# Moving state products, query transposes, output rows, table reads, squares and gates to other places in a retention and expert kernel

## The chip, the cores and the metric

The kernel runs on one core of a Trainium2 chip. The metric is device time of one execution in microseconds, median over the runs. Engines are named PE (TensorE's products), PEld (its weight loads), DVE (VectorE), ACT (ScalarE), POOL (GpSimd) and SP (SyncE, which here issues transfers); POOL issues the indirect transfers. PSUM banks hold TensorE's results.

## The reference

A linear attention with decay over 4 batches, 8 heads, 768 positions and 64 columns a head gives 3072 rows x of 512 columns. Each row chooses the expert with the largest cosine logit of eight, and passes through that expert's two layers (512 to 1024 to 512) with a gate.

```python
for t in range(S):
    state = gamma * state + k[:, :, t] (outer) v[:, :, t]
    y[:, :, t] = scale * q[:, :, t] @ state
x = y.transpose(0, 2, 1, 3).reshape(B * S, H * D)
logits = normed(x) @ normed(expert_emb).T / tau
expert_idx = argmax(logits);  gate_w = softmax(logits)[expert_idx]
for e in range(E):
    h = maximum(x[mask] @ w1[e], 0)
    out[mask] = gate_w[mask] * (h @ w2[e])
```

## The kernel before, in words

**Order.** All five engines run under a manual schedule: each executes its instructions in the order in which the code writes them, so moving a line moves its instructions past everything that the same engine, or the same transfer queue, does in between. An instruction that waits holds up all behind it on its engine.

**Attention.** 12 steps m (4 batches by 3 blocks of 256 positions) run in one loop. A step has two halves s of keys. For each: the product of keys and queries (`scores`, L357, banks psc), a product of the queries with the running state (`inter`, L410, banks py), VectorE's `masks` (L366) over the scores, and the product of masked scores and values (`intra`, L410). `state(m)` (L382) adds a block's keys times values into the banks pst, ACT's `state_copy` copies one of them, and VectorE's `state_sums` (L394 to L399) makes the state that the next step's `inter` reads. `transpose_k` and `transpose_q` (L330) turn the next step's keys and queries on TensorE into one of two banks pt; ACT copies them (L340, L346). `take` has ACT copy the step's result from py (L432); in the next step `logits_products` (L451) multiplies it with the turned embeddings, and `rows` turns it on VectorE (L437) and writes it to the x rows in DRAM (xd).

**Routing.** Steps are gathered in groups; when a group is over, `sums` (L469), `choose`, `count` (L496 to L500) and `ranks` find each row's expert and its place, and POOL's `place` writes the entries of 128 rows with one indirect transfer each (L529) into a table tbl in DRAM. Expert 0's first 288 rows ("early") are read from the table at step 10 and gathered (`early_gather`, L559, tile xge); the other 128 ("late", tile xr0) can be read only when the last group is placed.

**Weights.** An expert has eight pieces of 512 KB. `load_piece` (L183 to L191) starts the transfer of the next piece on SP into one of 3 tiles raw (pool rp). `split_cast` has ACT round it to whi (L210) and `low` has VectorE subtract to wlo (L215); `split` does both. Each product is three: xh with whi, xl with whi, xh with wlo. The tuples `LOADS` and `SPLITS` name the steps at which pieces are started and split during the attention.

**Experts.** `rows_T` (L577, L580) turns gathered rows of expert 0 on TensorE; for experts 1 to 7 rows are gathered (`gather_rows`, tile xr), written to DRAM scratch xs (`write_rows`) and read back in quarters (`read_quarters`, L912, tile xg), turned on VectorE and rounded (`x_turn`, L922 and L923), and `x_low` (L929) makes xl. `next_x(e, i)` does that for the next expert in three parts during the second layer, each with a weight split. `first_layer` (L228) and `hidden` (L234 on ACT, L235 on VectorE) give hh and hl; `layer2` (L939) and, for experts with 384 rows, `layer2_rows` (L981) give the output, which `finish` scales by the gate (L956) and POOL writes out (L963). `squares` (L262, ACT) and `gates` (L246 to L283, VectorE with one POOL instruction, L247, and one ACT instruction, L277) make the gates. `run(n)` puts the next n products of expert 0's first layer into the tail of the routing.

## Time and profile before

| | us |
|---|---|
| median of 3 runs | 455.42 |
| lowest and highest run | 452.3, 456.49 |
| the profiled execution, whole | 450.94 |
| its span in the trace | 449.1 |
| busy time of PE, DVE, ACT, POOL in it | 411.2, 255.5, 173.8, 168.7 |
| mean granted clock of TensorE | 0.975 |

The profiled execution lies 4.48 us under the median of the runs; 1.84 us of it lie outside the traced span. The granted clock is a share of full speed, of 2.4 GHz: 0.50 is 1.2 GHz. "Idle before" is time in which an engine stood, and the arrow names what ended it.

### The profile page before, as it was taken

To read this page: it belongs to the slowest core of one execution; us is meant where nothing else is said; L and a number is where in the kernel's file an instruction comes from. 1 tells how busy PE (TensorE), PEld (TensorE's weight loads), DVE (VectorE), ACT (ScalarE), POOL (GpSimd) and SP (SyncE) were. 2 spreads that over 40 slices of the span, in tenths; PEclk is the share of its full clock that TensorE was granted. 3 is DMA by queue.
4 is the path that set the end of the run, shared out by engine and by line. 5 is a ranking of instruction groups with operands and counts; after the bars stand their busy time and mean duration, and the time that the engine had idled before them with its cause. 6 is when DMAs were issued, how large, how long until landed. Compare 5 with 4: busy or idle time off the path is not lost.

```text
span 449.1 us, 11335 instructions
## 1 busy us (share of the span) xinstructions
PE 411.2 (92%) x4540; PEld 367.0 (82%) x4540; DVE 255.5 (57%) x543; ACT 173.8 (39%) x315; POOL 168.7 (38%) x171
## 2 busy tenths in 40 slices
PE   7889889998859979997999999999998997999993
PEld 4778767877636978896899999999998987989982
DVE  3454745655862925565856585378467558666410
ACT  3314333334342515345346346156237326525300
POOL 1743356665645242072440172143135065012011
PEclk9989999999996999999899999999999999999998
DMA  9998878888583468649886968778788697864001
GB/s 238 274 227 217 224 196 228 222 217 200 131 228 112 99 165 234 151 122 279 233 267 176 229 220 243 165 254 268 177 242 273 178 290 256 257 203 138 0 26 47
DMA packets 97966, 88.75 MB, mean 198 GB/s; under 512 B 11148, under 2 KB 79644, under 8 KB 97904
## 3 DMA queue, kind: packets, MB, share of 16 engines
q1 hardware_dynamic: 92832, 74.85, 62.6%
q0 software_dynamic: 4928, 13.04, 8.4%
q8 instruction: 37, 0.61, 0.6%
q14 instruction: 25, 0.20, 0.2%
q10 hardware_dynamic: 144, 0.05, 0.1%
HBM read 65.27 MB, written 18.87 MB: 187 GB/s over the span
## 4 chain that ended last, share of the span: by engine, by line
PE 38%; DMA 16%; SPq 15%; DVE 10%; issue 10%; POOL 6%; ACT 4%; POOLq 0%; DVEq 0%; ACTq 0%
SPq L951 8%; PE py L410 5%; DMA xg<-xs 5%; PE py L981 5%; PE psc L228 4%; PE pt L330 4%; PE pst L228 4%; DMA xr<-xd,gi 4%; PE psc L357 4%; DVE wlo L215 3%; PE py L228 3%; DMA xs<-xr 2%; PE psc L939 2%; ACT whi L210 2%; SPq L912 2%
## 5 line engine op out<-in xcount | busy, mean ns | idle before, releaser
L215 DVE TENSOR_TENSOR wlo<-raw,whi 128x1024 fp32r<-128x1024 f32 x61 | 73.8, 1213 | 24.4 <-ACT whi L210 23.6
L963 POOL DMA_INDIRECT out_dram<-og,si x29 | 35.8, 1234 | 118.5 <-DVE og L956 101.7
L210 ACT CAST whi<-raw 128x1024 fp32r<-128x1024 f32 x64 | 65.6, 1043 | 6.2 <-POOL si L556 5.3
L366 DVE TENSOR_TENSOR pm<-psc,cst 128x512 f32<-128x512 f32 x48 | 30.9, 686 | 34.8 <-PE psc L357 34.8
L923 ACT CAST xh<-xt 128x384 fp32r<-128x384 f32 (+4 forms) x28 | 14.5, 522 | 73.2 <-DVE xt L922 73.2
L318 POOL TENSOR_TENSOR hl<-wlo,cst 128x512 f32<-128x512 f32 x22 | 22.9, 1062 | 51.1 <-PE pt L451 29.5
L559 POOL DMA_INDIRECT xr<-xd,gi x26 | 34.7, 1336 | 8.5 <-issue 5.5
L228 PE MATMUL pst<-xl,whi 128*128 128x384 f32 (+5 forms) x96 | 32.9, 343 | 4.0 <-DVE xl L929 4.0
L357 PE MATMUL psc<-qT,kT 64*64 64x128 f32 x768 | 35.1, 282 | 1.2 <-DVE qT L346 0.9
L247 POOL TENSOR_TENSOR r<-r,half 128x4 f32<-128x4 f32 (+1 forms) x9 | 8.9, 993 | 67.1 <-DVE r L246 67.1
L228 PE MATMUL pst<-xh,whi 128*128 128x384 f32 (+5 forms) x96 | 32.7, 341 | 1.3 <-ACT whi L210 1.2
L228 PE MATMUL pst<-xh,wlo 128*128 128x384 f32 (+5 forms) x96 | 32.4, 338 | 0.0
L529 POOL DMA_INDIRECT tbl<-zt,sloti x24 | 24.7, 1028 | 14.1 <-issue 5.8
L357 PEld LDWEIGHTS psc<-qT,kT 64*64 64x64 f32 x768 | 25.2, 136 | 5.3 <-DVE parts L459 1.5
L228 PE MATMUL py<-xh,whi 128*128 128x384 f32 (+5 forms) x84 | 28.5, 339 | 0.0
L228 PE MATMUL py<-xl,whi 128*128 128x384 f32 (+5 forms) x84 | 28.4, 338 | 0.0
L228 PE MATMUL py<-xh,wlo 128*128 128x384 f32 (+5 forms) x84 | 28.3, 337 | 0.0
L939 PE MATMUL psc<-hh,whi 128*128 128x288 f32 (+4 forms) x80 | 27.5, 344 | 0.0
L922 DVE STREAM_TRANSPOSE xt<-xg 128x416 f32<-128x416 f32 (+1 forms) x28 | 15.5, 573 | 21.0 <-DMA xg<-xs 20.1
L939 PE MATMUL psc<-hl,whi 128*128 128x288 f32 (+4 forms) x80 | 27.2, 340 | 0.0
L939 PE MATMUL psc<-hh,wlo 128*128 128x288 f32 (+4 forms) x80 | 27.2, 339 | 0.0
L228 PE MATMUL psc<-xh,whi 128*128 128x384 f32 (+5 forms) x76 | 25.4, 334 | 0.0
(207 smaller groups left out, 1019.4 us busy)
## 6 DMA issues: line engine op xcount, KB each, us to landing
raw<-in_moe_w_dram SPq DMA_DIRECT2D x46, 512.0 KB
raw<-in_moe_w_dram SPq DMA_DIRECT2D x28, 256.0 KB
xd<-x SPq DMA_DIRECT2D x48, 128.0 KB
wlo<-in_k_dram SPq DMA_DIRECT2D x11, 512.0 KB
whi<-in_q_dram SPq DMA_DIRECT2D x11, 512.0 KB
xs<-xr SPq DMA_DIRECT2D x6, 768.0 KB
xg<-xs SPq DMA_DIRECT2D x16, 208.0 KB
whi<-in_v_dram SPq DMA_DIRECT2D x6, 512.0 KB
```

The source lines that it names most:

```text
L210: nc.scalar.copy(out=hv, in_=rv)
L215: eng.tensor_tensor(out=lv, in0=rv, in1=hv.bitcast(F32), op=ALU.subtract)
L228: nc.tensor.matmul(acc[:, :w], a[:, f], x[:, kt, cols], start=(n == 0), stop=(n == 3 * KT - 1))
L318: return eng.tensor_tensor(out=dst[:, h], in0=src[m % 3][:, h, s], in1=w[:, h], op=ALU.mult)
L357: nc.tensor.matmul(psc[a][u * 64:(u + 1) * 64, j], kTs[m][a * D:(a + 1) * D, sk, j, u * 64:(u + 1) * 64], q_cols(m, a, j, u), start=True, ...
L366: i = nc.vector.tensor_tensor(out=pm, in0=psc[a], in1=C("mask")[:, sk * P:(sk + 1) * P].unsqueeze(1).broadcast_to([P, KT, P]), op=ALU.mult)
L410: nc.tensor.matmul(pys[m][u][o * D:(o + 1) * D, j], lhsT, rhs, start=first, stop=True, skip_group_check=True)
L529: i = nc.gpsimd.indirect_dma_start(out=tbl[:, :], out_offset=bass.IndirectOffsetOnAxis(ap=sloti[:, n:n + 1], axis=0), in_=zt[:, n], in_off ...
L559: nc.gpsimd.indirect_dma_start(out=xr[:n, j, :], out_offset=None, in_=xd[:rows_, :], in_offset=bass.IndirectOffsetOnAxis(ap=gi[:n, e, at:a ...
L939: nc.tensor.matmul(acc[:, :c], a[:, f], x[:, kt, :c], start=(n == 0), stop=(n == 3 * FT - 1))
L951: nc.sync.dma_start(out=og[h * Q:(h + 1) * Q, :n, i * P:(i + 1) * P], in_=yt[i * Q:(i + 1) * Q, h:nb:NQ].rearrange("p n t a -> p n (t a)"))
L963: i = nc.gpsimd.indirect_dma_start(out=out[:, :], out_offset=bass.IndirectOffsetOnAxis(ap=si[:n, e, j:j + 1], axis=0), in_=og[:n, j, :], i ...
```

## The change

- **The step.** `state(m + 1)` and `state_copy` stand ahead of the second half's scores, behind `transpose_k(m + 1, 1)`, and not behind that half's masks. Both `transpose_q` stand in a row behind the second half's masks. `rows(m - 1)` stands behind `masks(psc, 1)` and `state_sums`. The logits of steps 0 and 1 are both computed at step 2, and two of the three embedding steps moved to the ends of steps 0 and 1, the third to step 2.
- **Weights.** The raw tiles are 4 instead of 3. The sixth and seventh load is at other steps, five pieces instead of six are split in the attention, and the subtractions stand behind `take(m)` (one at step 10 on POOL).
- **The end of the attention.** `rows_T` of the early rows stands behind both intra products and `take`, and not ahead of them. `place` takes 2, 3 or 4 entries at a step where it took 2 or 4.
- **Expert 0.** The reads of the table for the late rows and for experts 1 and 2 stand ahead of all weight loads there. One load waits for the late gather, three follow. Three instead of two column blocks of the second layer stand ahead of the late rows' transposes.
- **Experts.** `finish` runs on ACT instead of VectorE. `squares(e + 1)` stands in the second layer of expert e instead of its first. The gates of e are computed in e's own first layer. Splits stand at ft 0, 1, 3, 5 and 6 of the first layer instead of ft 0, 2, 4, 6 and one in the second. `next_x` turns the fourth quarter one part earlier, and its last `x_low` stands ahead of the last split.

```diff
-LOADS = (8, 8, 9, 9, 10, 10, 11, 11)
-SPLITS = (9, 9, 10, 10, 11, 11)
+LOADS = (8, 8, 9, 9, 9, 11, 11, 11)
+SPLITS = (9, 9, 10, 10, 11)
-    rp = ctxw.enter_context(tc.tile_pool(name="rp", bufs=3))
+    rp = ctxw.enter_context(tc.tile_pool(name="rp", bufs=4))
...
         if nxt:
             transpose_k(m + 1, 1)
-        if m == 1:
+            state(m + 1)
+            state_copy(m + 1)
+        if m == 2:
             next(emb_steps)
-        if m:
-            pl = logits_products(m - 1)
-            logits_rows(m - 1, pl)
-        if nxt:
-            transpose_q(m + 1, 0)
+        for i in () if m < 2 else (0, 1) if m == 2 else (m - 1,):
+            pl = logits_products(i)
+            logits_rows(i, pl)
         psc = scores(m, 1, range(1))
         inter(m, 1)
         scores(m, 1, range(1, KT), psc)
-        if m:
-            rows(m - 1)
         i = masks(psc, 1)
...
         if nxt:
-            state(m + 1)
-            state_copy(m + 1)
+            state_sums(m + 1)
+        if m:
+            rows(m - 1)
+        if nxt:
+            transpose_q(m + 1, 0)
             i = transpose_q(m + 1, 1)
...
         if m == NM - 1:
             run_all(choose(done, z))
             run_all(add_counts(done))
-            for kt in range(KT):
-                rows_T(xge, EROWS, kt, slice(0, EARLY), bank(f"pst{kt}") if kt < 2 else None)
         intra(m, 1)
...
         take(m)
+        if m == NM - 1:
+            for kt in range(KT):
+                rows_T(xge, EROWS, kt, slice(0, EARLY), bank(f"pst{kt}") if kt < 2 else None)
+        for low in lows:
+            low()
...
-    load_expert(1)
-    load_piece()
-    load_piece()
     nc.sync.dma_start(out=tb[:, 0, 3], in_=tbl[EARLY:CAPS[0], :])
     slots(1)
+    slots(2)
...
+    load_piece(late_rows)
+    for _ in range(3):
+        load_piece()
-    for dt in range(2):
+    for dt in range(3):
         acc = layer2(0, dt, hh0, hl0, EARLY)
...
     def finish(e, j, n, og, src=None):
-        nc.vector.tensor_scalar(out=o, in0=o if src is None else src, scalar1=gt[:n, e, j:j + 1], scalar2=None, op0=ALU.mult)
+        nc.scalar.activation(out=o, in_=o if src is None else src, func=AF.Copy, scale=gt[:n, e, j:j + 1])
...
         elif i == 1:
             x_low(e, 1)
+            x_turn(e, 2)
             lo = split_cast()
-            x_turn(e, 2)
+            x_low(e, 2)
+            x_turn(e, 3)
             lo()
-            x_low(e, 2)
-            load_piece()
         else:
-            x_turn(e, 3)
+            x_low(e, 3)
             split()
-            x_low(e, 3)
...
-            if ft % 2 == 0:
+            if ft in (0, 1, 3, 5, 6):
                 split()
                 load_piece()
-            if nxt:
-                if ft in (2, 3):
-                    squares(e + 1, ft - 2)
...
+                if dt < 2:
+                    squares(e + 1, dt)
```

**VectorE in an attention step (step 3).** pm is a masked half of the scores, parts the turned logits, s the state sums, x the turned output rows. Before:

```order
L366 TENSOR_TENSOR pm_1394<-psc_1370,cst_61 128x512
L366 TENSOR_TENSOR pm_1396<-psc_1371,cst_61 128x512
L459 STREAM_TRANSPOSE parts<-pt 128x256
L437 STREAM_TRANSPOSE x<-yT 128x4x4x32 x2
L366 TENSOR_TENSOR pm_1457<-psc_1428,cst_61 128x512
L366 TENSOR_TENSOR pm_1459<-psc_1429,cst_61 128x512
L394 TENSOR_TENSOR s_1507<-pst_1280,tB 128x256
L399 TENSOR_TENSOR s_1509<-pst_1280,tB 128x256
```

In the changed kernel:

```order
L368 TENSOR_TENSOR pm_1394<-psc_1370,cst_61 128x512
L368 TENSOR_TENSOR pm_1396<-psc_1371,cst_61 128x512
L461 STREAM_TRANSPOSE parts<-pt 128x256
L368 TENSOR_TENSOR pm_1477<-psc_1455,cst_61 128x512
L368 TENSOR_TENSOR pm_1479<-psc_1456,cst_61 128x512
L396 TENSOR_TENSOR s_1481<-pst_1230,tB 128x256
L401 TENSOR_TENSOR s_1483<-pst_1230,tB 128x256
L439 STREAM_TRANSPOSE x<-yT 128x4x4x32 x2
```

The two instructions of L437 (now L439), which make the output rows, moved from ahead of the second pair of masks to behind the state sums.

**TensorE at the end of the attention (step 11 into expert 0).** xge holds the gathered early rows, pm and wlo are masked scores and values. Before, the last scores of the step, the routing sums and the row transposes, with the intra products behind:

```order
L357 MATMUL psc_2453<-qT,kT 64x128 x2
L469 MATMUL pt<-parts,cst_61 32x32 x4
L577 MATMUL pst_2512<-ident,xge 128x128 x2
L577 MATMUL pst_2512<-ident,xge 128x32
L577 MATMUL pst_2518<-ident,xge 128x128 x2
L577 MATMUL pst_2518<-ident,xge 128x32
L577 MATMUL pt<-ident,xge 128x128 x2
L577 MATMUL pt<-ident,xge 128x32
L577 MATMUL pt<-ident,xge 128x128 x2
L577 MATMUL pt<-ident,xge 128x32
L410 MATMUL py_2428<-pm_2485,wlo 64x128
```

In the changed kernel:

```order
L412 MATMUL py_2427<-pm_2442,wlo 64x128
L579 MATMUL pst_2562<-ident,xge 128x128 x2
L579 MATMUL pst_2562<-ident,xge 128x32
L579 MATMUL pst_2568<-ident,xge 128x128 x2
L579 MATMUL pst_2568<-ident,xge 128x32
L579 MATMUL pt<-ident,xge 128x128 x2
L579 MATMUL pt<-ident,xge 128x32
L579 MATMUL pt<-ident,xge 128x128 x2
L579 MATMUL pt<-ident,xge 128x32
L233 MATMUL psc_2595<-xh,whi 128x288
L233 MATMUL psc_2595<-xl,whi 128x288
L233 MATMUL psc_2595<-xh,wlo 128x288
```

The row transposes (L577, now L579) moved from ahead of the intra products (L410, now L412) to directly ahead of expert 0's first product (now L233).

**SP's queue before expert 0's late rows.** tb is what is read from the table, raw the weights, cnti the order of the experts. Before:

```order
L186 DMA raw<-in_moe_w_dram 64x1024
...
L186 DMA raw<-in_moe_w_dram 64x1024
L857 DMA tb<-tbl 128x10
L834 ISA
L834 DMA tb<-tbl 128x4x10
L188 ISA
L188 DMA raw<-in_moe_w_dram 128x1024
L169 TENSOR_LOAD cnti
L169 ISA x2
L834 ISA
L834 DMA tb<-tbl 128x4x10
```

In the changed kernel:

```order
L857 DMA tb<-tbl 128x10
L172 TENSOR_LOAD cnti
L172 ISA x2
L837 ISA
L837 DMA tb<-tbl 128x4x10
...
L837 ISA
L837 DMA tb<-tbl 128x4x10
L1165 TENSOR_LOAD cnti
L1165 ISA x2
L191 ISA
L191 DMA raw<-in_moe_w_dram 128x1024
```

The reads of the table (L857 and L834, now L857 and L837) moved from behind and between the weight loads to ahead of them.

## Rows read from the trace of the kernel before

**Rows 1.** The page's first list, its line on TensorE: busy time, share of the span, instructions; the other engines stand behind it.

```profile
PE 411.2 (92%) x4540; PEld 367.0 (82%) x4540; DVE 255.5 (57%) x543; ACT 173.8 (39%) x315; POOL 168.7 (38%) x171
```

**Rows 2.** Busy time of each engine by stretches of the span. Columns: the stretch and its length, busy time and number of instructions of PE, PEld, DVE, ACT and POOL, the mean granted clock of TensorE, the busy share of the DMA engines and what they moved in GB/s. The stretches are the attention without its first steps and its end, and the first and the second layer of expert 1.

```profile
33.40:103.70 70.30, 64.47 (x1747) 52.49 (x1743) 39.27 (x89) 25.13 (x47) 38.52 (x38) 1.00 0.82 215
...
187.00:205.90 18.90, 18.65 (x98) 17.86 (x97) 10.67 (x21) 10.21 (x23) 9.98 (x9) 1.00 0.52 152
205.90:230.40 24.50, 21.39 (x98) 19.03 (x97) 17.98 (x35) 11.73 (x19) 11.04 (x10) 0.93 0.90 246
```

**Rows 3.** The same view, by stretches cut where the granted clock changes (columns as in rows 2); between them, from 30.4 us to 446 us, it was 1.00.

```profile
27.00:30.00 3.00, 3.00 (x68) 3.00 (x72) 1.33 (x3) 0.59 (x1) 2.72 (x3) 0.50 0.91 229
...
132.80:143.00 10.20, 7.61 (x81) 5.31 (x81) 2.37 (x7) 2.64 (x5) 5.31 (x3) 0.50 0.58 187
...
167.00:170.20 3.20, 3.20 (x10) 2.52 (x9) 1.89 (x4) 2.10 (x5) 2.89 (x5) 0.50 0.63 183
...
214.80:218.00 3.20, 3.20 (x9) 3.07 (x10) 2.23 (x5) 1.00 (x2) 2.02 (x2) 0.50 1.09 290
```

**Rows 4.** What TensorE waited for, over the whole span: tile and line of the waiting product, releaser, total in us, number of waits, the longest one.

```profile
PE pst L577 <- DMA xge<-xd,gi: 5.0, 2, 4.7
PE pst L228 <- DVE xl L929: 4.0, 4, 1.3
...
PE py L939 <- DVE hl L235: 2.7, 4, 1.4
PE pt L577 <- DMA xr<-xd,gi: 1.8, 1, 1.8
...
PE pst L228 <- ACT whi L210: 1.2, 1, 1.2
```

**Rows 5.** The timeline of one attention step, TensorE (a query transpose, the state product, the other query transpose, the first intra product) and then VectorE (the second half's masks): start in us, duration, engine, line, operation, and in square brackets the idle time before it and what ended it.

```profile
36.92 0.63 PE L330 MATMUL pt<-ident,hh 128*128 128x128 f32 x4 [0.20 <-ACT kT L340]
...
38.84 1.11 PE L382 MATMUL pst<-wlo,hl 64*64 64x64 f32 x64
39.88 0.66 PE L330 MATMUL pt<-ident,hh 128*128 128x128 f32 x4
40.46 1.98 PE L410 MATMUL py<-pm,whi 64*64 64x128 f32 x64
...
39.05 1.29 DVE L366 TENSOR_TENSOR pm<-psc,cst 128x512 f32<-128x512 f32 x2 [0.62 <-PE psc L357]
```

**Rows 6.** The first two steps, as timeline: on SyncE the transfer of the second block of v, on TensorE a query transpose and the state product that reads that block, and in the second step the two embedding products with their waits.

```profile
11.29 0.39 SPq L304 DMA_DIRECT2D wlo<-in_v_dram  x1
...
13.64 0.66 PE L330 MATMUL pt<-ident,hh 128*128 128x128 f32 x4
...
15.80 1.16 PE L382 MATMUL pst<-wlo,hl 64*64 64x64 f32 x64
...
24.50 0.44 PE L607 MATMUL pt<-ident,xge 8*128 8x8 f32 x4 [1.03 <-ACT kT L340]
...
25.75 0.63 PE L451 MATMUL pt<-yT,enT 128*32 128x256 f32 x6 [0.81 <-DVE enT L608]
```

**Rows 7.** The end of the attention, as timeline of TensorE: the first row transpose of the early rows (L577), the first intra product behind them (L410) and the first product of expert 0 (L228).

```profile
135.06 0.47 PE L577 MATMUL pst<-ident,xge 128*128 128x128 f32 x1 [4.69 <-DMA xge<-xd,gi]
...
139.16 1.98 PE L410 MATMUL py<-pm,wlo 64*64 64x128 f32 x32
...
143.14 0.40 PE L228 MATMUL psc<-xh,whi 128*128 128x288 f32 x1
```

**Rows 8.** Expert 0's late rows, as timeline: SyncE's read of the table for them (L857), POOL's late gather, and TensorE with the late rows' transposes.

```profile
156.82 0.53 SPq L857 DMA_DIRECT2D tb<-tbl  x1
...
162.28 1.14 POOL L559 DMA_INDIRECT xr<-xd,gi  x1 [0.99 <-DMA tb<-tbl]
...
165.73 0.44 PE L577 MATMUL pt<-ident,xr 128*128 128x128 f32 x2 [1.80 <-DMA xr<-xd,gi]
166.74 0.67 PE L577 MATMUL pt<-ident,xr 128*128 128x128 f32 x2 [0.57 <-DVE xl L580]
```

**Rows 9.** Expert 1's turn from the first to the second layer, as timeline: ACT with one of the squares of expert 2's rows (L262), then two products of the second layer with their waits.

```profile
206.40 0.63 ACT L262 ACTIVATE sq<-xr 32x512 bf16<-32x512 f32 x1 [1.08 <-DMA xr<-xd,gi]
...
210.34 0.46 PE L939 MATMUL py<-hl,whi 128*128 128x416 f32 x1 [0.97 <-DVE hl L235]
...
213.14 0.45 PE L939 MATMUL py<-hl,whi 128*128 128x416 f32 x1 [1.40 <-DVE hl L235]
```

**Rows 10.** The turn from expert 3 to expert 4, as timeline: ACT's three weight casts in a row, VectorE's last xl, and the product that waits for it.

```profile
301.07 2.94 ACT L210 CAST whi<-raw 128x1024 fp32r<-128x1024 f32 x3
...
303.29 0.56 DVE L929 TENSOR_TENSOR xl<-xt,xh 128x392 fp32r<-128x392 f32 x1
...
303.90 0.45 PE L228 MATMUL pst<-xl,whi 128*128 128x392 f32 x1 [1.20 <-DVE xl L929]
```

**Rows 11.** Groups of instructions by line and shape over the span: line, engine, operation, tiles, shapes, number, busy time in us, mean ns of one, idle time before them and its releasers.

```profile
L432 ACT COPY yT<-py 128x512 f32<-128x512 f32 x24 | 12.9, 590 | 20.5 <-PE py L410 20.5
...
L262 ACT ACTIVATE sq<-xr 128x512 bf16<-128x512 f32 x22 | 13.8, 629 | 4.9 <-DMA xr<-xd,gi 4.6
...
L956 DVE TENSOR_SCALAR og<-og,gt 128x512 f32<-128x512 f32 x14 | 6.2, 476 | 10.2 <-DMA og<-yt 6.4 <-DMA xg<-xs 3.7
...
L956 DVE TENSOR_SCALAR og<-py,gt 128x512 f32<-128x512 f32 x5 | 3.7, 749 | 11.2 <-PE py L981 11.2
```

More of the change, by code (lines that the diff above doesn't have):

```diff
@@ L187, in load_piece @@
         elif j < 4:
-            nc.sync.dma_start(out=r, in_=w1r[ds(e * DM + j * P, P), :])
+            i = nc.sync.dma_start(out=r, in_=w1r[ds(e * DM + j * P, P), :])
+            if behind is not None:
+                after(i, behind)
         else:
@@ L785, in retention_moe @@
         lows = [split_cast() for _ in range(SPLITS.count(m))]
-        if nxt:
-            state_sums(m + 1)
-        if m == 0:
-            next(emb_steps)
+        if m < 2:
             next(emb_steps)
@@ L843, in retention_moe @@
     run_all(add_counts(g))
-    rows(m)
-    run(12)
+    run(9)
     pr = count(g)
@@ L850, in retention_moe @@
     place(range(span(g).start, span(g).stop))
+    rows(m)
     for _ in range(9):
@@ L863, in retention_moe @@
     split()
-    load_piece()
-    slots(2)
     for j, n in EROWS:
         square(xge, n, j, j)
+    run(12)
+    split()
     run(DF)
@@ L1018, in retention_moe, with turn_hidden @@
             split()
-            load_piece()
             run_all(gsteps)
     read_quarters(1)
-    acc = layer2(0, 2, hh0, hl0, EARLY)
-    split()
     load_piece()
-    y_turn(2, acc, yt0, EARLY)
-    for f in range(2):
+    load_piece()
+    def turn_hidden(f):
         ps = pt_()
@@ L1049, in retention_moe @@
     squares(1)
-    gsteps = gates_of(1)
-    next(gsteps)
-    split(nc.gpsimd)
-    load_piece()
-    run_all(gsteps)
     indices(P, 2, slice(0, NG))
@@ L1114, in retention_moe @@
                 out_rows(pend[1], pend[2], ft, pend[3])
-            if nxt:
-                if ft in (2, 3):
-                    squares(e + 1, ft - 2)
-                if ft == 3:
-                    read_quarters(e + 1)
-                if ft == 4:
-                    gsteps = gates_of(e + 1)
-                    next(gsteps)
-                if ft >= 6:
-                    for _ in range(4):
-                        next(gsteps, None)
+            if nxt and ft == 3:
+                read_quarters(e + 1)
+            if ft == 1:
+                gsteps = gates_of(e)
+                next(gsteps)
+            if ft > 2:
+                for _ in range(3):
+                    next(gsteps, None)
             if ft == FT - 2 and c % P:
```

37 lines of the change are left out of this document (16 added, 21 removed).

## The prediction, made before the changed kernel was run

> **What bounds the kernel now.** I read the page's first list first: TensorE is busy for 411.2 of 449.1 us [rows 1], no other engine for more than 57%. So the time is TensorE's work, plus its idle time, plus what its work costs more where it runs at half clock; a change of order can only win from the last two. Next the busy time by stretches: the reader is to see that the attention's long part has little to give (64.47 busy of 70.30 us), and that expert 1's second layer takes 24.50 us where its first layer, with as many products (98), takes 18.90 [rows 2]. Then the stretches of half clock, cut until each is uniform: 3.0, 10.2, 3.2 and 3.2 us, and no others [rows 3]. Each of the last three began in or behind idle time of TensorE. Last the list of its waits: 5.0 us for the early gather, 4.0 for xl of the next expert in four waits, 2.7 for hl, 1.8 for the late gather, 1.2 for a cast weight [rows 4]. These five entries are most of what an order can remove, and the change moves something at each.
>
> **The change part by part.** The sum is made against the profiled execution, 450.94 us.
>
> *Step 0.* state(1) now runs where q's transpose stood, at about 13.64 us instead of 15.80 [rows 6]. It reads the second block of v, whose transfer was issued at 11.29; at 15.80 it did not wait [rows 6], so the block landed by then, and nothing shows when. The new wait lies between 0 (landed by 13.64) and 2.2 us. I take **+2.2**, because the loads of this stretch run back to back and the row at 15.80 is the only one that shows it landed. Scores and query transposes behind it wait with it.
>
> *Embeddings.* In step 1 the embedding products wait 1.03 and 0.81 us [rows 6]; their chain now has a step more to run in. Between 0 and -1.84; I take **-1.4**, leaving one short wait at step 2, where logits of two steps now stand in a row.
>
> *The step.* Before, the second half's masks (1.29 us, 0.2 us behind the last scores) were covered by the state product and one query transpose: from 38.84 to 40.46, and intra began without idle time [rows 5]. Now only two transposes (0.63 and 0.66) cover 0.2 + 1.29 + 0.1, so intra waits some 0.3 us; the 0.20 us ahead of the first transpose goes [rows 5]. Net +0.1, and +0.25 where pt's two banks are then not free in time. For ten steps 0 to +2.5; I take **+1.2**. The moved output rows (two transposes on VectorE) stand behind state_sums, which are off TensorE's way for the rest of the step; their DMA reaches SP some 3 us later in the step, ahead of the gather by several steps except at the last, which is in the next term.
>
> *End of the attention.* The early transposes waited 4.69 us for the gather and then ran at half clock, as did both intra products: expert 0 began at 143.14 [rows 3, 7]. Now intra and count come first and the transposes last. The gather's landing (135.06) stays the bound, since it hangs on the table, not on TensorE. The 12 transposes took 4.1 us at half clock (135.06 to 139.16), so 2.05 at full; xl of the last then lies uncovered, some 0.57 us as in the one row of this kind [rows 7, 8]. Expert 0 begins at 135.06 + 2.05 + 0.57 = 137.7 at full clock (-5.5), at 139.7 at half (-3.4). Idle time of 1 to 2 us ahead of the transposes remains, and where 1.80 + 0.57 us of it stand, half clock followed [rows 3, 8]. I take **-3.4** and keep -5.5.
>
> *Late rows.* SP's read of the table was issued at 156.82 behind weight loads, and the transposes waited 1.80 us [rows 8]. The read now stands ahead of the loads, and a third column block of the second layer (24 products; 96 of 416 columns take 18.9 us [rows 2], so 24 of 288 some 3.3 us) stands ahead of the transposes. 1.80 us go, and with them the half clock behind (3.2 us, worth 1.6 to 1.7) [rows 3]: **-3.5**, with -1.8 and -4.1 (the 0.57 too) as ends. The price is weight loads that start some 5 us later; expert 1's first pieces are split in expert 0's last 15 us, which is their cover.
>
> *Expert 1's second layer.* hl came late (0.97 and 1.40 us) because ACT stood in squares that waited for the gather of expert 2's rows, with hidden's ACT work behind them; half clock followed [rows 3, 9]. The squares now stand behind the last hidden, the gates no longer come between, and one split fewer stands there. 24.50 becomes 18.90: **-5.6** [rows 2]; the end near nothing is rival B.
>
> *Turns between experts.* ACT did three weight casts in a row (2.94 us), VectorE's last xl stood behind a subtraction that waited for them, and the next expert's product waited 1.20 us [rows 10]. x_low now stands ahead of the last split, its x_turn a part earlier, and a fourth raw tile lets the transfers start earlier. The four waits for xl (4.0) and one for whi (1.2) go [rows 4]: **-5.0**, ends 0 and -5.2.
>
> *finish on ACT.* 14 instructions of 476 ns and 5 of 749 ns leave VectorE [rows 11]. ACT's nearest rows are 590 ns (from PSUM) and 629 ns (with a sum) [rows 11]. In a quarter of a second layer (18.9 / 4 = 4.7 us) ACT then does two finishes, two squares, two xh and one cast, 5 us or a little more, where VectorE had room; the third and fourth quarter have almost nothing, so xh of the next expert is late by under 1 us where it has 7 to spare. **0** inside. The last finish behind the last product is 749 ns now and some 0.6 then: -0.1. The Trainium skill (ScalarE: Activation LUTs, What ACT_TABLE_LOAD costs) gives an activation 186 ns plus 0.833 ns for a column and 93 ns more for each scale or bias held in a tile, an estimate of 706 ns here. No run here shows that form; by it the last finish would win nothing and the sum would be 0.1 us less.
>
> Sum: 2.2 - 1.4 + 1.2 - 3.4 - 3.5 - 5.6 - 5.0 - 0.1 = -15.6. 450.94 - 15.6 = 435.3 for an execution like the profiled one. The median of the three runs stands 4.48 above that one, so 455.42 - 15.6 = **439.8**, which is the forecast.
>
> **The rivals.**
>
> *A. More is won.* Full clock at the end of the attention (2.1 more), step 0's block landing early (2.2 more), the half clock at 27 us gone (1.5). About 434. For it: each is an end of a bound above. Against: they need not come together. It is inside the forecast's own range, 433 to 446.
>
> *B. Expert 1's inputs become late.* Four weight loads now stand behind the late gather and share the DMA engines with its rows, xs and xg; the engines were 0.90 busy in expert 1's second layer [rows 2]. If pieces come late, TensorE waits at expert 1's first products instead of in its second layer. Then most of the 5.6 is lost: 445. For it: the late gather was issued only at 162.28 [rows 8], and these loads cannot start ahead of it. Against: 0.52 busy in expert 1's first layer [rows 2], so there is room to catch up.
>
> *C. The waits at the turns stay.* ACT now carries finish and squares in the same second layer; if xh of the next expert slips behind casts as at 301.07 [rows 10], the -5.0 is lost: 445. With B, 450, which is the change that moves waits and wins only at the attention's end and the late rows.
>
> *D. Slower: the clock falls in the attention.* The change adds a wait in nearly every step, small but regular, and a longer one in step 0. A stretch of half clock of 3.2 us costs 1.6; the attention's 92 us from 33.4 to 125 ran at full clock throughout. To be slower than before by more than the bound, 15.6 + 4.5 us must be lost, so some 40 us of the attention at half clock; if it ran wholly so, it would be 80 us or more longer. For it: 10.2 us at half clock followed the 4.69 us wait [rows 3, 7], and the clock returned only when expert 0 began. Against: the step's present wait of 0.20 us [rows 5] never did that, and 0.3 us is like it. The time would be 470 and more. The Trainium skill (TensorE: Matmul & The Clock Gate, Part 1, The HAM clock gate) says "the default state is throttled, and activity releases the throttle"; the trace agrees, as rows 3 and 7 show half clock behind a wait and full clock in the dense products of expert 0. By that rule the attention, which is the least dense part, is where it would begin.
>
> *E. It was not the order.* If the waits of [rows 4] only follow the DMA engines (0.90 and 0.82 busy in [rows 2]), earlier work waits for the same transfers, and about 5 us remain: 451.
>
> **How the numbers follow.** Forecast with A 0.60, B 0.13, C 0.11, D 0.07, E with B and C together 0.09. A measurement of this kernel can tell about 1% from no change, 4.5 us: faster is under 450.9, slower over 460. The forecast, B and C are faster, and E is half so; D is slower: 0.84, 0.09, 0.07. The range leaves out D and the outer part of E above, and the lowest of A below: 432 to 449.
>
> **What would show it.** Right: the first product of expert 0 at 137 to 141 us; no wait over 0.6 us ahead of the late rows' transposes; expert 1's second layer under 20 us; no wait of over 1 us for xl at the turns; granted clock at half in at most two stretches behind 30 us. Wrong: a wait of 2 us at TensorE's first products of expert 1 (B), ACT's finish ahead of a late xh (C), half clock between 33 and 125 us (D). A state product at 14 us without a wait would make the first term wrong by 2.2.

## The result, and the profile after

The changed kernel takes 436.44 us (median of 4 runs, 433.7 to 442.5) where the kernel before takes 454.26 in the same set: a ratio of 0.959, 95% interval 0.951 to 0.966. The forecast was 439.8. The profiled execution took 433.7 us, its span 431.9 us, 17.2 less than before. Ratios are made from the faster runs of each kernel, and the profiles of a0_change and x4_raw3 come from runs over 1.5% longer than their kernel's fastest, so their lengths in the table below are not compared.

The page's first list, its line on TensorE:

```profile
PE 404.6 (94%) x4540; PEld 364.6 (84%) x4540; DVE 240.7 (56%) x517; ACT 190.2 (44%) x343; POOL 155.3 (36%) x169
```

TensorE is idle for 27.3 us of its span where it was idle for 37.9 [rows 1]; its busy time fell by 6.6 us for the same 4540 products, most of it half clock that went. What it waited for (columns as in rows 4):

```profile
PE pt L547 <- ACT kT L342: 4.9, 1, 4.9
PE pst L384 <- DMA wlo<-in_v_dram: 2.5, 1, 2.5
...
PE pst L233 <- DVE xl L930: 1.0, 3, 0.5
...
PE pt L579 <- DVE xl L582: 0.6, 1, 0.6
```

The gathers and hl are off the list [rows 4], xl has 1.0 left of 4.0, all of it in expert 1's first layer. At the head of it stands a wait of 4.9 us that was not there before, for a copy of kT by ACT. By stretches (columns as in rows 2): the new wait and what follows it, and expert 1's two layers:

```profile
113.60:118.50 4.90, 0.01 (x1) 0.10 (x1) 2.62 (x3) 3.55 (x5) 1.96 (x2) 0.67 0.75 145
118.50:130.00 11.50, 11.31 (x273) 9.26 (x272) 6.91 (x16) 4.40 (x8) 2.59 (x3) 0.84 0.58 148
...
181.30:201.40 20.10, 19.12 (x98) 17.74 (x97) 13.84 (x28) 12.37 (x24) 7.45 (x7) 1.00 0.75 228
201.40:219.50 18.10, 18.10 (x97) 17.94 (x96) 9.23 (x17) 10.69 (x20) 6.13 (x6) 1.00 0.86 225
```

Expert 1's second layer takes 18.1 us where it took 24.5, its first layer 20.1 where it took 18.9 [rows 2]. The new wait brings half clock with it, from 115.3 to 122.1 us, so 0.84 on the mean of the 11.5 us behind it; nowhere else behind 30 us was the clock at half before 429 us. By the starts of the first products of the experts and steps in the two timelines (us):

| stretch | before | after | change | predicted |
|---|---|---|---|---|
| to the first intra product of step 2 | 40.46 | 40.86 | +0.4 | +0.8 |
| steps 3 to 9, by the same product | 70.51 | 69.92 | -0.6 | +1.2 |
| step 10 | 11.81 | 15.68 | +3.9 | none |
| from there to expert 0's first product | 20.4 | 14.3 | -6.1 | -3.4 |
| expert 0 | 43.88 | 40.55 | -3.3 | -3.5 |
| expert 1 | 43.3 | 38.2 | -5.1 | -5.6 |
| experts 2 to 6 with their turns | 178.1 | 171.7 | -6.4 | -5.0 |
| expert 7 and the end | 40.7 | 40.7 | 0 | -0.1 |
| sum | 449.1 | 431.9 | -17.2 | -15.6 |

The sum was near the mark. The experiments ask whether the reasons were.

### The profile page after: what moved, and what is told of

It reads as the page before. It is cut to its first block, busy times and chain, and to the rows that moved or that the text cites. A ratio compares the mean times of both kernels' runs of the same rounds, so it can differ in the third digit from the quotient of the medians.

```text
span 431.9 us, 11314 instructions
## 1 busy us (share of the span) xinstructions
PE 404.6 (94%) x4540; PEld 364.6 (84%) x4540; DVE 240.7 (56%) x517; ACT 190.2 (44%) x343; POOL 155.3 (36%) x169
## 4 chain that ended last, share of the span: by engine, by line
PE 68%; DMA 9%; issue 8%; DVE 5%; SPq 4%; POOL 2%; ACT 2%; POOLq 0%; DVEq 0%; ACTq 0%
PE pst L233 10%; PE py L233 9%; PE psc L940 8%; PE psc L233 7%; PE py L412 5%; PE psc L359 5%; PE py L940 4%; PE pst L940 4%; PE pt L335 4%; PE py L982 4%; PE psc L982 4%; DMA wlo<-in_v_dram 3%; PE pst L384 3%; DMA xr<-xd,gi 2%; DVE x L439 1%
## 5 line engine op out<-in xcount | busy, mean ns | idle before, releaser
L220 DVE TENSOR_TENSOR wlo<-raw,whi 128x1024 fp32r<-128x1024 f32 x63 | 76.7, 1218 | 22.4 <-ACT whi L215 21.6
L964 POOL DMA_INDIRECT out_dram<-og,si x29 | 29.5, 1016 | 150.1 <-ACT og L957 96.5
L233 PE MATMUL pst<-xl,whi 128*128 128x384 f32 (+5 forms) x96 | 32.8, 342 | 1.0 <-DVE xl L930 1.0
L233 PE MATMUL pst<-xh,whi 128*128 128x384 f32 (+5 forms) x96 | 32.5, 339 | 0.0
L233 PE MATMUL pst<-xh,wlo 128*128 128x384 f32 (+5 forms) x96 | 32.4, 338 | 0.0
L233 PE MATMUL py<-xh,whi 128*128 128x384 f32 (+5 forms) x84 | 28.5, 339 | 0.0
L233 PE MATMUL py<-xl,whi 128*128 128x384 f32 (+5 forms) x84 | 28.4, 338 | 0.0
L233 PE MATMUL py<-xh,wlo 128*128 128x384 f32 (+5 forms) x84 | 28.3, 337 | 0.0
L233 PE MATMUL psc<-xh,whi 128*128 128x384 f32 (+5 forms) x76 | 25.4, 334 | 0.0
L233 PE MATMUL psc<-xh,wlo 128*128 128x384 f32 (+5 forms) x76 | 25.4, 334 | 0.0
L348 ACT COPY qT<-pt 128x512 f32<-128x512 f32 x22 | 11.8, 589 | 30.4 <-PE pt L335 30.4
L233 PE MATMUL psc<-xl,whi 128*128 128x384 f32 (+5 forms) x76 | 25.2, 331 | 0.0
L940 PE MATMUL psc<-hh,whi 128*128 128x416 f32 (+4 forms) x72 | 24.6, 341 | 0.0
```

The costliest lines, as they stand in the source:

```text
L220: eng.tensor_tensor(out=lv, in0=rv, in1=hv.bitcast(F32), op=ALU.subtract)
L233: nc.tensor.matmul(acc[:, :w], a[:, f], x[:, kt, cols], start=(n == 0), stop=(n == 3 * KT - 1))
L940: nc.tensor.matmul(acc[:, :c], a[:, f], x[:, kt, :c], start=(n == 0), stop=(n == 3 * FT - 1))
L964: i = nc.gpsimd.indirect_dma_start(out=out[:, :], out_offset=bass.IndirectOffsetOnAxis(ap=si[:n, e, j:j + 1], axis=0), in_=og[:n, j, :], i ...
```

## The experiments

Twelve kernels ran, in three sets of four. The first set ran on a chip that takes 466.12 us for the kernel before and stops TensorE in the attention for its own instructions (the intra products' waits named "issue": 5.4 to 6.6 us in all, against 0.2 to 3.7 in every other run), so its times are compared within the set. The table gives, for the runs whose experts are compared, the first product of expert 0 in its profile, the length of expert 0, of expert 1 and of experts 2 to 6 together, the median, and the ratio to the kernel before of the same set.

| run | expert 0 begins | 0 | 1 | 2 to 6 | median, ratio |
|---|---|---|---|---|---|
| before | 143.1 | 43.9 | 43.3 | 178.1 | 454.26 |
| the change | 140.7 | 40.5 | 38.2 | 171.7 | 436.44, 0.959 |
| a0_change (second set) | 147.9 | 43.6 | 39.1 | 171.7 | 438.41, 0.965 |
| b_raw4 (second) | 148.0 | 42.2 | 43.2 | 178.7 | 453.49, 1.002 |
| x5_next_x (second) | 143.0 | 40.7 | 38.3 | 181.6 | 444.73, 0.981 |
| x1_again (second) | 142.2 | 42.9 | 38.3 | 172.3 | 437.25, 0.964 |
| c1_three_edits (third) | 137.4 | 40.9 | 38.3 | 174.2 | 431.24, 0.948 |
| x6_squares (third) | 142.4 | 40.9 | 39.7 | 171.7 | 436.28, 0.958 |
| x7_loads_first (third) | 142.1 | 46.6 | 38.3 | 173.1 | 440.57, 0.969 |
| x3_finish_dve (third) | 140.8 | 40.6 | 37.9 | 187.0 | 451.02, 0.992 |
| x4_raw3 (first) | 159.6 | 45.0 | 43.8 | 181.0 | 469.77, none |

**The new wait: loads at step 7 (x1_loads7 on the first chip, x1_again on the second).**

```diff
-LOADS = (8, 8, 9, 9, 9, 11, 11, 11)
+LOADS = (7, 7, 9, 9, 9, 11, 11, 11)
```

> The changed kernel with its first two weight loads at the end of step 7 instead of step 8 (LOADS = 7,7,9,9,9,11,11,11). Theory S: TensorE's new 4.90 us wait at 113.6 us comes from the queue of SyncE: the moved output rows put their four writes ahead of the weight loads, these start at 106.2 instead of 102.8 us, ACT's two casts of step 9 wait 3.38 and 0.50 us for them, and the copies behind the casts hold TensorE's bank. Then the casts do not wait here, the 4.90 becomes 0.7 or less, the half clock behind it goes, expert 0 begins at 135 to 137 us instead of 140.7, and the time is 431 (5 less). Rival P: the wait hangs on VectorE's longer row of work (the moved row transposes ahead of choose), so it stays at 4 to 5 us and the time at 436.

> The first two weight loads at the end of step 7, as in the first set, now beside the changed kernel itself. Theory S (SyncE's queue): where the changed kernel waits 4 to 5 us at 113 us, this one waits under 1.3 there, expert 0 begins 3 to 5 us earlier and the time is 3 to 5 us under it; where the changed kernel does not wait there, the two agree within 2 us. Rival P (VectorE's longer row): the wait stays.

> The changed kernel as it is, to stand beside the others of this set. On a chip where the kernel before takes 452 to 456 us: 434 to 438, with a wait of 4 to 5 us of TensorE at 113 us. On a chip where the kernel before takes 465 to 467, as the first set's did, TensorE's steps of the attention stop for its own instructions and the casts of step 9 find their weights landed: 450 to 453, with a wait under 1.3 us there.

First the place in the changed kernel, as timeline: SyncE's issues of the first two pieces (L186), ACT with the casts, the two copies of `take` (L434) and kT (L342), and TensorE's product that waits for a bank pt:

```profile
106.21 6.87 SPq L186 DMA_DIRECT2D raw<-in_moe_w_dram  x8
...
114.42 1.04 ACT L215 CAST whi<-raw 128x1024 fp32r<-128x1024 f32 x1 [3.38 <-DMA raw<-in_moe_w_dram]
115.96 1.04 ACT L215 CAST whi<-raw 128x1024 fp32r<-128x1024 f32 x1 [0.50 <-DMA raw<-in_moe_w_dram]
116.91 1.06 ACT L434 COPY yT<-py 128x512 f32<-128x512 f32 x2
117.86 0.60 ACT L342 COPY kT<-pt 128x512 f32<-128x512 f32 x1
...
118.51 0.17 PE L547 MATMUL pt<-cum,ones 128*128 128x8 f16 x1 [4.90 <-ACT kT L342]
```

The kernel before, at the same place:

```profile
102.83 6.28 SPq L183 DMA_DIRECT2D raw<-in_moe_w_dram  x8
...
111.37 1.99 ACT L210 CAST whi<-raw 128x1024 fp32r<-128x1024 f32 x2
```

The four writes of the output rows, next ahead in SyncE's queue but for one load, begin at 101.93 instead of 97.93. The first of the eight weight transfers is issued at 106.21 instead of 102.83, ACT's first cast waits until 114.42, the copies of `take` and kT stand behind the two casts, and TensorE gets its bank at 118.51. In the first set the question couldn't be decided: the slower attention gave the weights time in every kernel, with and without the edit (waits there of 0.7 to 1.2 us; 453.51 us, 0.973). On the second chip it could. With the loads at step 7, as timeline of SyncE and ACT, and from the list of waits:

```profile
98.58 6.55 SPq L186 DMA_DIRECT2D raw<-in_moe_w_dram  x8
...
112.88 2.01 ACT L215 CAST whi<-raw 128x1024 fp32r<-128x1024 f32 x2
...
PE pt L547 <- ACT kT L342: 1.1, 1, 1.1
...
PE pt L500 <- DVE oh L491: 3.7, 3, 3.0
```

The casts do not wait, and the 4.73 us that a0_change waits at this place (5.07, 5.05 and 5.11 in x5, x6 and x3) is 1.1 here; step 10 takes 10.45 us instead of 16.44 (15.7 to 16.7 in the others that wait). So the wait hangs on when the weights land, as theory S has it, and rival P falls. That the output writes made the weights late is read from the order and the times of SyncE's queue; no run puts them back on a chip that shows the wait. It hangs on a few us: in x7_loads_first the loads start at 106.12, as in the change, but half clock from 103.4 to 106.9 held TensorE back; the casts, reached at 113.65, found their weights landed, and the wait was 1.0. The time of x1_again moved by only 1.2 us, less than the runs scatter: the last line shows a new wait of 3.0 us one step later, for the routing's count, with half clock behind it.

**The output rows in their old place in three steps (x9_rows_early, first chip).**

```diff
+        if m in (7, 8, 9):
+            rows(m - 1)
         i = masks(psc, 1)
...
-        if m:
+        if m and m not in (7, 8, 9):
             rows(m - 1)
```

> The changed kernel with the output rows of steps 6, 7 and 8 (computed in steps 7, 8 and 9) ahead of the second half's masks again, all else as in the change. Theory S: the writes leave SyncE about 3 us earlier, the weight loads start at about 103, ACT's casts wait under 0.5 us and the 4.90 us wait falls to 1 or less; in return VectorE's masks of these three steps come 1.3 us later, with only two transposes to cover them, so the steps cost 1.0 to 1.3 us more each. Net 434 to 437. Rival P: the wait stays at 4 or more and the steps cost 3 to 4 us more in all: 439 to 440.

451.66 us, 0.968, beside 453.51 for x1_loads7. No wait of 4 us is there (0.81), but neither was it in x2 and x4 of that set, where the rows stand as in the change. So this run does not tell S from P.

**State(1) behind the masks in step 0 (x2_state0, first chip).**

```diff
             transpose_k(m + 1, 1)
-            state(m + 1)
-            state_copy(m + 1)
+            if m:
+                state(m + 1)
+                state_copy(m + 1)
...
+        if nxt and not m:
+            state(1)
+            state_copy(1)
```

> The changed kernel with state(1), its copy behind the second half's masks again in step 0 alone, as before the change. Theory W: the 2.46 us wait of step 0 is a loss of its own, so that every later step begins 2.5 to 3.5 us earlier, and the time is 433. Rival L: the loads of the next blocks set the pace of the first two steps (TensorE's step 1 took 14.05 us before and 9.19 in the changed kernel, and both reach step 2 within 0.9 us of each other), so what step 0 wins step 1 gives back: the first intra product of step 2 stays within 0.7 us of 40.85 and the time at 436.

The wait of 2.5 to 3.1 us that the others of the set have in step 0 is gone, and its first intra product comes at 18.27 us instead of 19.79 to 22.27. In step 1 that is lost again: the first intra product of step 2 stands at 40.42, beside 39.85 to 41.67. That is rival L's outcome, but not its reason: TensorE waits for no load in step 1. It stops once, among the scores:

```profile
27.61 0.69 PE L359 MATMUL psc<-qT,kT 64*64 64x128 f32 x4 [2.33 <-issue]
```

With it half clock begins, for 3.4 us. No run shows what the stop waits for (x9 has 1.1 us of it, x1_loads7 and x4 0.3 or less). The time is 452.92, 0.963, the lowest of the set's three ratios, and the change itself did not run there. So whether step 0's wait costs time stays open.

**Three edits together (c1_three_edits).** Loads at step 7; and for the wait that came up behind it, two edits more.

```diff
-LOADS = (8, 8, 9, 9, 9, 11, 11, 11)
+LOADS = (7, 7, 9, 9, 9, 11, 11, 11)
...
-        if m:
+        if m and nxt:
             rows(m - 1)
...
-        if m == NM - 2:
-            lows.pop()(nc.gpsimd)
         if m == NM - 1:
             run_all(choose(done, z))
             run_all(add_counts(done))
+            rows(m - 1)
```

> The changed kernel with three edits at the end of the attention: the first two weight loads at step 7, step 10's POOL subtraction on VectorE with the others, and the output rows of step 10 behind choose in step 11. Theory: with the loads at step 7 step 10 took 10.44 us instead of 16.44, but 3 to 4 us of it came back as a wait of 2.96 us for the routing's count (a VectorE instruction of 0.19 us took 2.18 beside POOL's subtraction, and the row transposes of 1.29 us stood ahead of choose) and as half clock behind it. With both removed from that place the wait is 0.5 us or less, expert 0 begins 13 to 15 us behind step 10's first intra product (19.0 with the loads alone), and the time is 0.950 to 0.957 of before (0.965 for the change, 0.964 with the loads alone). Rival: the early gather is the bound there (its third transfer is issued at 132.7 in any order), TensorE waits for it instead, and the ratio stays at 0.960 to 0.966.

What x1_again showed at that wait, VectorE and then POOL:

```profile
133.79 0.19 DVE L483 TENSOR_TENSOR zt<-pt,m 128x32 f32<-128x32 f32 x1
134.02 2.18 DVE L486 SCALAR_TENSOR_TENSOR w<-zt,cst 128x32 f32<-128x32 f32 x1
136.23 0.19 DVE L489 TENSOR_REDUCE wmn<-w 128x4 f32<-128x32 f32 x1
...
133.79 2.35 POOL L220 TENSOR_TENSOR wlo<-raw,whi 128x1024 fp32r<-128x1024 f32 x1
```

VectorE's L486 takes 2.18 us and ends just behind POOL's subtraction (133.79 + 2.35); its neighbours take 0.19. In c1_three_edits, without POOL's subtraction there, it takes 0.19 too. TensorE there, from the routing's count to expert 0's first product:

```profile
133.79 0.18 PE L500 MATMUL pt<-oh,tri 128*128 128x32 f16 x1
...
135.62 0.79 PE L579 MATMUL pst<-ident,xge 32*128 32x32 f32 x4 [0.19 <-DMA xge<-xd,gi]
...
137.42 0.40 PE L233 MATMUL psc<-xh,whi 128*128 128x288 f32 x1
```

Count does not wait, a transpose waits 0.19 us for the gather, and expert 0 begins 14.4 us behind step 10's first intra product (19.0 in x1_again), at full clock. 431.24 us, 0.948 with 95% interval 0.943 to 0.954: the fastest version here, below the theory's range; experts 2 to 6 give back 2.5 us of what the attention won. The rival (the gather as bound at 0.960 to 0.966) falls; the 0.19 us say that the gather is next in line. The two edits beside the loads were made together, so their shares are not told apart.

**The fourth raw tile taken away (x4_raw3, first chip), and given to the kernel before (b_raw4).**

```diff
-    rp = ctxw.enter_context(tc.tile_pool(name="rp", bufs=4))
+    rp = ctxw.enter_context(tc.tile_pool(name="rp", bufs=3))
```

> The changed kernel with 3 raw weight tiles instead of 4. Theory R: the fourth tile is what lets weights come early, so that casts do not stand in a row at the turns between experts; with 3, waits of about 1.2 us come back at the turns to experts 4, 5 and 6 (3 to 5 us in all) and the attention's casts wait as much as now or more: 440 to 442. Rival O: the order in next_x alone took the waits away, and the turns stay without waits over 0.6 us: 436 to 437.

> The kernel before with one number changed: 4 raw weight tiles instead of 3. Theory R (the fourth tile is the larger part of what the experts gain): with 3 tiles in the new order the experts behind expert 0 took 295 + 13 us, so with 4 in the old order the four waits for xl at the turns (4.0 us) and the half of expert 1's lateness go, and the time falls by 5 to 10 us. Theory RO (tile and order win only together, since in the old order ACT's casts stand in a row ahead of xh and the squares ahead of hidden whatever is in the tiles): it falls by 0 to 3 us.

The new order with 3 tiles takes 469.77 us; its least run, 461.2, lies 8 to 12 us over the least runs of the other three of its set (448.9 to 453.0). Two waits in its profile: ACT in expert 1, and one line of TensorE's waits.

```profile
229.42 1.04 ACT L215 CAST whi<-raw 128x1024 fp32r<-128x1024 f32 x1 [7.09 <-DMA raw<-in_moe_w_dram]
230.37 0.51 ACT L239 ACTIVATE hh<-pst 128x416 fp32r<-128x416 f32 x1
...
PE py L940 <- ACT hh L239: 2.5, 1, 2.5
```

ACT stands 7.09 us in a cast whose piece has not landed, hidden is behind it, and TensorE waits 2.5 us for hh. So the tile is needed. But it does nothing by itself: the old order with 4 tiles takes 453.49 us, a ratio of 1.002 (0.994 to 1.010), with the old waits for xl and hl:

```profile
PE pst L228 <- DVE xl L929: 3.8, 3, 1.3
...
PE py L939 <- DVE hl L235: 2.7, 4, 1.4
```

Theory RO holds: the tile wins nothing without the new order, and the new order loses much of its win without the tile.

**next_x in the old order (x5_next_x).**

```diff
             x_low(e, 1)
-            x_turn(e, 2)
             lo = split_cast()
-            x_low(e, 2)
-            x_turn(e, 3)
+            x_turn(e, 2)
             lo()
+            x_low(e, 2)
         else:
-            x_low(e, 3)
+            x_turn(e, 3)
             split()
+            x_low(e, 3)
```

> The changed kernel with next_x in the order of before (the fourth quarter turned in the third part, its x_low behind the last split), 4 raw tiles. Theory R: the tile carries the turns, so the product at a turn waits under 0.6 us and the time is within 1 us of the changed kernel. Theory O: the order carries them, waits of 1.2 to 1.3 us for xl come back at four turns or more, and the time is 4 to 6 us over the changed kernel.

444.73 us, 6.3 over a0_change (its ratio 0.016 higher): theory O. The waits at the turns are back, up to 1.3 us each, in the list of TensorE's waits:

```profile
PE pst L233 <- DVE xl L930: 5.3, 7, 1.3
...
PE pst L233 <- ACT whi L215: 1.3, 1, 1.3
```

Experts 2 to 6 take 9.9 us more: 5.6 are these waits (6.6, less the 1.0 left in the change), and most of the rest is the clock, which behind the two waits at the turn to expert 4 was 0.50 from 299.5 to 306.2 us, worth 3.4.

**finish on VectorE again (x3_finish_dve).**

```diff
-        nc.scalar.activation(out=o, in_=o if src is None else src, func=AF.Copy, scale=gt[:n, e, j:j + 1])
+        nc.vector.tensor_scalar(out=o, in0=o if src is None else src, scalar1=gt[:n, e, j:j + 1], scalar2=None, op0=ALU.mult)
```

> The changed kernel with finish on VectorE again. As predicted (term of nothing): within 1.5 us of the changed kernel, no wait over 0.7 us at any turn. Rival C turned round: with finish off ACT the casts and xh come 1.2 us earlier in each second layer, the turns gain and the time is 2 us or more under the changed kernel; or VectorE becomes late with xl and wlo and 1.2 us waits return at two turns or more: 2.5 us over it.

The largest miss: 451.02 us, 0.992, 13 to 15 us over the change's two medians. Expert 0 and 1 take the same; experts 2 to 6 take 15.3 us more: 5.8 of waits (2.9 for wlo, 2.6 for whi, 0.3 for xl), and two stretches of half clock, 295.8 to 302.4 and 371.0 to 377.5 us, worth 3.3 each. In expert 3's second layer, as timeline of VectorE (the turn of the next expert's rows, then the second pair of finishes) and POOL, and a line of TensorE's waits:

```profile
286.82 1.11 DVE L923 STREAM_TRANSPOSE xt<-xg 128x416 f32<-128x416 f32 x2 [3.19 <-DMA xg<-xs]
...
290.65 0.83 DVE L957 TENSOR_SCALAR og<-og,gt 128x512 f32<-128x512 f32 x2
...
291.37 1.44 POOL L964 DMA_INDIRECT out_dram<-og,si  x1 [5.45 <-DVE og L957]
...
PE pst L233 <- ACT whi L215: 2.6, 2, 1.4
```

The changed kernel at the same place, ACT's second pair of finishes and POOL:

```profile
283.78 1.33 ACT L957 ACTIVATE og<-og,gt 128x512 f32<-128x512 f32 x2
...
284.78 0.97 POOL L964 DMA_INDIRECT out_dram<-og,si  x1 [3.71 <-ACT og L957]
```

On VectorE the second finishes stand behind the row turns, which wait for rows from the scratch; on ACT they are done 7 us earlier. POOL's output transfers wait for them, and the gather of the rows for the expert after next stands on POOL behind those: its rows come late (for expert 4, SyncE reads them back at 279.89 instead of 273.98), so the next expert's turn is late, and with it the next finish. The loop is read from the two timelines; no run breaks it at one place, and the experts lose unevenly (expert 4 and 6 6.6 us each, the others 0.3 to 1.3). Rival C turned round named the 1.2 us waits (1.4 is there), not this loop.

**squares in the first layer again (x6_squares).** In this kernel the squares of the next expert overwrite those from which the present expert's gates are then made, so the gates are partly made from other rows; the work is the same.

```diff
+            if nxt and ft in (2, 3):
+                squares(e + 1, ft - 2)
...
-                if dt < 2:
-                    squares(e + 1, dt)
...
-                    if j < 2:
-                        squares(e + 1, j)
```

> The changed kernel with squares(e + 1) in the first layer again (ft 2 and 3). Theory: at expert 1 the squares wait on ACT for the gather of expert 2's rows, hidden's ACT work comes late, and TensorE waits 2 us or more around the turn from expert 1's first to second layer, which takes 4 to 6 us more with the half clock behind; the other experts take the same within 0.5 us each. Time 4 to 6 us over the changed kernel (ratio 0.974 to 0.978 of before). Rival: the lateness came from the splits and the gates in the same place, which stay moved; then no wait over 0.6 us comes back and the time is within 1 us of the change.

436.28 us, 0.958: no loss that can be told, and no wait over 0.6 us comes back in expert 1. The rival holds. Expert 1 takes 39.7 us instead of 38.2, but by stretches (columns as in rows 2) its second layer takes the same 18.1 us:

```profile
186.30:189.70 3.40, 3.36 (x10) 3.21 (x11) 1.25 (x2) 3.31 (x10) 0.00 (x0) 0.51 0.39 90
...
204.80:222.90 18.10, 18.10 (x97) 17.93 (x97) 9.93 (x16) 8.21 (x12) 8.00 (x9) 1.00 0.94 248
```

The 1.5 us lie in the half clock of the first line, which was over before the first square began. ACT's first square in expert 1 still waits, but the gather that it waits for is earlier in the expert (which begins at 183.2 here). ACT's square, and POOL's first of four transfers:

```profile
194.12 0.63 ACT L267 ACTIVATE sq<-xr 128x512 bf16<-128x512 f32 x1 [2.16 <-DMA xr<-xd,gi]
...
190.03 1.16 POOL L561 DMA_INDIRECT xr<-xd,gi  x1 [18.05 <-DMA og<-yt]
```

POOL in the kernel before, where expert 1 begins at 187.0:

```profile
192.03 1.02 POOL L247 TENSOR_TENSOR r<-r,half 128x4 f32<-128x4 f32 x1 [20.89 <-DVE r L246]
193.02 2.40 POOL L215 TENSOR_TENSOR wlo<-raw,whi 128x1024 fp32r<-128x1024 f32 x1
...
196.02 1.15 POOL L559 DMA_INDIRECT xr<-xd,gi  x1 [0.28 <-POOL gi L553]
```

There the gates' instruction and a weight subtraction of 2.40 us, both of expert 1, stood on POOL ahead of the gather, which began 9.0 us into the expert; now it begins 6.8 us into it. So what was predicted of the squares came from other parts of the change: this earlier gather, the gates, the split, or the fourth tile (without it a cast there waits 7.09 us). No run tells these apart, so which it was stays open.

**Two weight loads ahead of the table reads (x7_loads_first).**

```diff
+    load_expert(1)
+    load_piece()
+    load_piece()
     nc.sync.dma_start(out=tb[:, 0, 3], in_=tbl[EARLY:CAPS[0], :])
...
-    for _ in range(3):
-        load_piece()
+    load_piece()
```

> The changed kernel with two of expert 0's four weight loads ahead of the table reads again. Theory: the read of the late rows' entries waits on SyncE behind them, the late gather is issued 3 to 5 us later, TensorE waits 0 to 2 us for it (the third column block covers 3.3 us) and expert 0 takes up to 3 us more. Rival: the loads themselves come 5 us earlier, which helps the turn to expert 1 (0.9 to 1.2 us of waits there), and the time stays within 1.5 us of the changed kernel.

440.57 us, 0.969. SyncE's read of the table, POOL's late gather and the first gather of expert 1's rows, and a line of TensorE's waits:

```profile
158.82 0.52 SPq L860 DMA_DIRECT2D tb<-tbl  x1
...
164.65 1.14 POOL L561 DMA_INDIRECT xr<-xd,gi  x1 [1.02 <-DMA tb<-tbl]
...
166.39 1.11 POOL L561 DMA_INDIRECT xr<-xd,gi  x1 [0.28 <-POOL gi L555]
...
PE pst L233 <- ACT xh L927: 3.4, 1, 3.4
```

The changed kernel's read and gathers:

```profile
151.33 0.35 SPq L857 DMA_DIRECT2D tb<-tbl  x1
...
154.87 1.15 POOL L561 DMA_INDIRECT xr<-xd,gi  x1 [1.54 <-DMA tb<-tbl]
...
156.95 1.11 POOL L561 DMA_INDIRECT xr<-xd,gi  x1 [0.28 <-POOL gi L555]
```

The late gather comes 9.8 us later (8.4 counted from expert 0's first product), and TensorE still waits nothing for it: the third column block covers it, not the early read. What the read's place does is one queue on: the gather of expert 1's rows stands behind the late one on POOL and comes as much later, so expert 1's first product waits 3.4 us for xh, with half clock (0.51) for 3.3 us behind it. Expert 0 is 5.6 to 6.0 us longer than in the other kernels of its set, but only this wait of 3.4 belongs to the edit. Most of the rest is half clock in its first products, which came out of the attention (0.50 from 137.7 us on), ahead of the loads:

```profile
142.10:147.80 5.70, 5.70 (x27) 4.33 (x26) 2.64 (x5) 0.81 (x2) 0.98 (x1) 0.50 0.30 108
```

## Why the prediction was right, and where its reasons were not

The time, its range and its sign were right, and the rivals B, C, D and E did not set the time. But the sign that was named for D came: half clock between 33 and 125 us, from 115.3 to 122.1, worth 3.4 us, behind one long wait and not behind a small one in each step. By the steps:

- **Step 0 (+2.2).** The wait is there, 2.46 us, as priced. Step 0's first intra product comes 4.0 us later (21.50, before 17.48), with half clock behind the wait. **Embeddings (-1.4)**: their waits are gone but for 0.4, and with them the half clock at 27 us [rows 3]; step 1 takes 9.2 us instead of 14.1. Both steps together moved by +0.4. What paces them is not shown (x2_state0).
- **The step (+1.2).** -0.6: the masks' uncovered 0.3 us did not show as a sum.
- **End of the attention (-3.4).** -6.1, near the other bound of -5.5, because full clock came back. But ahead of it lay +3.9 that no term held, and the two belong together: with step 10 late, TensorE came behind the gather's landing and did not wait for it. Expert 0 begins at 140.7, inside the 137 to 141 forecast; c1_three_edits, without the wait, comes to 137.4, beside the 137.7 worked out for full clock. The failed sentence is that the moved rows' transfers reach SP some 3 us later in the step, "ahead of the gather by several steps": it named the delay and looked for its victim at the gather. What stood next in SyncE's queue were the weight loads, and behind them ACT's casts, its copies, and TensorE's bank. A wait of 4.69 us [rows 7] was traded for one of 4.90, with half clock behind either.
- **Late rows (-3.5).** -3.3. x7_loads_first leaves the third column block as the cause, by elimination; no run takes it out. The early table read, which I gave beside it, pays at expert 1's first product.
- **Expert 1 (-5.6).** -5.1: -6.4 in the second layer and +1.3 in the first, where waits for xl (1.0) came that no term held. The reason given, the squares' place, does not carry it: with the squares back in the first layer the second takes the same 18.1 us (x6_squares). Before, they did wait for the gather [rows 9]; with the gather earlier their place no longer mattered. Which of the moved gates, the split, the earlier gather and the fourth tile did it is open.
- **Turns (-5.0) and finish (0).** -6.4 together; the waits of 5.0 us behind expert 1 are all gone. The parts do not add: without the tile, without the order of next_x, or without finish on ACT, all of it or more is lost (6 to 15 us each), and the tile alone wins nothing. To cost finish I weighed busy times against a quarter of a layer, where its value is who waits behind it. Its duration was right in size: by line over the span,

```profile
L957 ACT ACTIVATE og<-og,gt 128x512 f32<-128x512 f32 x14 | 9.5, 716 | 13.3 <-DMA og<-yt 10.2 <-DMA xg<-xs 3.1
L957 ACT ACTIVATE og<-py,gt 128x512 f32<-128x512 f32 x5 | 3.4, 684 | 9.8 <-PE py L982 9.8
```

The Trainium skill (ScalarE: Activation LUTs, What ACT_TABLE_LOAD costs) led to an estimate of 706 ns; the trace agrees, with 716 from SBUF and 684 from PSUM.

Against the terms, +3.9 at step 10 stands beside -1.8 in the steps, -2.7 at the attention's end and -1.4 at the turns. That the sum came within 1.6 us is in part luck: the forecast was nearer than its reasons.

## What to carry to other kernels

When a step is moved, follow its transfers down their queue to the next one in it, and from that to who waits for it: here four writes put 4.0 us later made weight loads 3.4 us late, and that became 4.9 us of TensorE. Parts that close a loop (a free tile, an order of casts, the engine that finishes outputs) do not add: the tile won nothing alone (1.002), and taking out any one of the three lost 6 us or more. So undo each from the full version as well as adding it to the old one. And test the reason given for a term where its number came out right: here that of the squares did not hold. An instruction's engine is to be judged by what stands ahead of it and what waits behind it, not by its duration.

## What was unexpected of the hardware

One VectorE instruction of 0.19 us (L486) took 2.18 beside a POOL subtraction and ended with it, while the one ahead of it took its usual 0.19; in the changed kernel masks and row transposes beside the same subtraction took their usual 1.29. The kernel before has a second case, 0.16 us alone, beside the POOL subtraction that runs from 193.02 to 195.42:

```profile
193.30 2.13 DVE L251 TENSOR_TENSOR r<-r,ssq 128x4 f32<-128x4 f32 x1
```

The Trainium skill (SBUF — State Buffer, SBUF: two separate sides) says that a VectorE instruction with two SBUF inputs and a POOL instruction that reads SBUF exclude each other for its whole length; the trace agrees, since L486 and L251 read two tiles in SBUF, the others one at most. And two chips differ: on the first set's, expert 0 began at 153.5 us or later where the same order began it at 140.7 to 147.9 elsewhere, with the waits named "issue" in the intra products; no run here shows why.
